# A decode kernel's tail: 22 extra TensorE products, and an output in two column halves instead of four quarters

## The chip, the cores and the metric

The kernel runs on one core of one Trainium2 chip. The metric is device time in microseconds (us). The time before is 196.53 us, the median of three runs (196.53 to 196.76).

## The reference

One decode step for four sequences. A layer norm of `x` (4 x 512) feeds two branches whose results are added to `x`: attention over the last W = 4096 cached positions with 32 query heads in 8 key/value groups, and a gated feed-forward block.

```
xn = _layernorm(x)
q  = xn @ wq                                  # 4 x 4096, 32 heads of 128
k, v = the last 4096 positions of the caches  # 8 groups, 4 query heads each
o  = softmax(q k^T / sqrt(128)) v             # 4 x 4096
out = x + o @ wo + (silu(xn @ w_gate) * (xn @ w_up)) @ w_down
```

All inputs and the output are bf16. Weights and caches together are 81 MB, which are read once.

## The kernel before, in words

SyncE's queue loads everything in one fixed order: `wq`, `w_gate`, `w_up`, then for each of the eight key/value groups 4 MB of keys and 4 MB of values into two buffers each (`kbuf`, `vbuf`), then `w_down` (into `wg_sb`), then `wo` (into the first `kbuf`, free by then). `wo` comes in five chunks of its 32 row blocks, `ROWS`: blocks 0-15, 16-21, 22-28, 29-30 and 31. Each chunk has its own semaphore, `d_wo[0]` to `d_wo[4]`. All five are issued at L249, long before the end, and land in order.

TensorE's program for a key/value group is: transpose the keys (L418), multiply them with the queries (L427), sum and weight the values (L518, L436), shift the scores (L535) and fold partial sums (L539). ScalarE and VectorE copy, take the maxima and exponentials. This loop is not touched by the change.

After the last group comes the tail (block `t_tail`), which is straight code. TensorE works in order, so each of its waits holds up everything behind it:

- The attention result of all groups, `oT`, is transposed (L559) and spread by four products (L562). VectorE turns that into `oP` with four instructions (L384, L388) and signals `s_opc`. Meanwhile TensorE multiplies `guT` with `w_down` into `part_ps` (L569, 14 products).
- TensorE waits for `s_opc` and `d_wo[0]`, then multiplies `oP` with `wo` row blocks 0 to 21 (L577, `EARLY` = 22 products of 512 columns). At block 16 it waits for `d_wo[1]`. These products go to four groups of 32 partitions in turn (`32 * k`, `k = (j + 3) % 4`). Products on different groups run beside one another.
- VectorE copies the lower 64 partitions of `part_ps` to `part` (L391), ScalarE the upper 64 (L271). Each adds one to `s_ptc`.
- TensorE waits for both, folds the four partition groups of `part` into `acc_ps` with an fp32 matrix `fold` (L582), and adds row blocks 22 to 31 directly (L589), with waits for `d_wo[2]`, `d_wo[3]`, `d_wo[4]` at blocks 22, 29 and 31. `acc_ps` is one PSUM bank, `ps_S[2]`. The four column quarters of the output stand in its four partition groups, so each row block takes four products of 128 columns.
- After `s_acc`, VectorE casts quarters 0 and 1 to bf16 into `y` (L394), ScalarE quarters 2 and 3 (L274), 4 x 128 each. SyncE waits for both and writes `y` out (L251).

Two tiles matter for the change beside these: `ones` (128 x 128 of ones, bf16) and `P` (the exponentials, bf16), both last written long before the tail. `ps_kt[1]` is a PSUM bank that the loop uses for transposed keys, and that the tail does not use. In the profile's names, `kbuf<-in_A_wo_dram` is a `wo` chunk's transfer, `ps_s` any of the four `ps_S` banks, `PEld` the load of a product's stationary matrix.

Of the kernel before, what the change touches and what calls it, by code (L numbers as in the profile page):

```python
# [10 lines left out]
def bass_parallel_sum__sliding_block_cached__swiglu_ffn__decode_kernel(  # L11
# [12 lines left out]
    B, _, D = A_x.shape  # L24
    _, HKV, Sk, Dh = A_k_cache.shape
# [10 lines left out]
    NC = D // 128  # L36
# [19 lines left out]
    WO = KB[0][:].rearrange("p t d -> p (t d)").rearrange("p (j n) -> p j n", n=D)  # L56
# [11 lines left out]
    P = sb("p", [128, NT, CQ], BF16)  # L68
# [16 lines left out]
    OP = sb("oP", [128, 32, 32], BF16)  # L85
    guT = sb("guT", [128, NF, 32], BF16)
    part = sb("part", [128, D], FP32)
    y = sb("y_sb", [B, D], BF16)
# [3 lines left out]
    ones = sb("ones", [128, 128], BF16)  # L92
    I48 = sb("i48", [48, CQ], FP32)
    Lsel = sb("lsel", [128, 128], BF16)
    fold = sb("fold", [128, 32], FP32)
# [6 lines left out]
    ps_S = [ps("ps_s%d" % s, [128, 512], FP32) for s in range(NB)]  # L102
    ps_kt = [ps("ps_kt%d" % s, [128, 512], FP32) for s in range(3)]
# [13 lines left out]
    part_ps = ps_S[0]  # L117
    rt_ps = kt_ps[0][:, 0, :]
    op_ps = ps_S[1][:].rearrange("p (b q j) -> p b q j", b=B, q=4)
    acc_ps = ps_S[2]  # L120

    def sem(name):
        return nc.alloc_semaphore(name=name)
# [47 lines left out]
    s_y = sem("s_y")  # L171
# [82 lines left out]
    def run_scalar(eng):  # L254
        eng.dma_start(X[:], x_ap).then_inc(d_x, 16)
        eng.wait_ge(s_var, 1)
        eng.activation(st_std[:], st_var[:], ACT.Sqrt).then_inc(s_std, 1)
        eng.wait_ge(s_q, 1)
        eng.copy(qs[:, 1, :], ps_S[1][:]).then_inc(s_qs, 1)
        eng.wait_ge(s_g, 1)  # L260
        eng.activation(ex, gate_ps[:], ACT.Exp, scale=-1.0).then_inc(s_ex, 1)
        with eng.Fori(0, HKV) as i:
            for n in BY_ACT:
                eng.wait_ge(s_tr[n], i + 1)
                eng.copy(KT[n % 8][:], kt_ps[n % 3]).then_inc(s_ev[n], 1)  # L265
            for q in range(NB):
                eng.wait_ge(s_sh[q], i + 1)
                eng.activation(P[:, q * TB:(q + 1) * TB, :], S_ps[q], ACT.Exp,  # L268
                               scale=SCALE).then_inc(s_xp[q], 1)
        eng.wait_ge(s_pt, 1)  # L270
        eng.copy(part[64:128, :], part_ps[64:128, :]).then_inc(s_ptc, 1)  # L271
        eng.wait_ge(s_acc, 1)
        for n in (2, 3):
            last = eng.copy(y[:, 128 * n:128 * n + 128], acc_ps[32 * n:32 * n + B, 0:128])  # L274
        last.then_inc(s_y, 1)

    def run_vector(eng):
        me = bass.OrderedEngineSet([eng.engine])
# [106 lines left out]
        for q in range(1, 4):  # L385
            eng.drain()
            dst = opf[:] if q < 3 else OP[:, :, 0:B].rearrange("p j b -> p b j")
            last = eng.scalar_tensor_tensor(dst, op_ps[:, :, q, :], quarter[:, q:q + 1], opf[:], ALU.mult, ALU.add)  # L388
# [1 line left out]
        eng.wait_ge(s_pt, 1)  # L390
        eng.tensor_copy(part[0:64, :], part_ps[0:64, :]).then_inc(s_ptc, 1)  # L391
        eng.wait_ge(s_acc, 1)
        for n in (0, 1):
            last = eng.tensor_copy(y[:, 128 * n:128 * n + 128], acc_ps[32 * n:32 * n + B, 0:128])  # L394
        last.then_inc(s_y, 1)

    def run_tensor(eng):
        mm = eng.matmul
# [5 lines left out]
        def now(reg, lo=1, hi=16 * HKV):  # L404
            return eng.snap(reg, min_val=lo, max_val=hi, donate=True)

        def step(reg, by, op=ALU.add):
            nc.regs_alu(reg, reg, by, op=op)
# [24 lines left out]
        def pv(e):  # L433
            for u in range(NT // 2):
                k = u % 4
                last = mm(o4_ps[32 * k:32 * k + 32, :], P[:, 2 * u:2 * u + 2, :].rearrange("p t c -> p (t c)"),  # L436
                          VB[e][:, 2 * u:2 * u + 2, :].rearrange("p t d -> p (t d)"),
                          start=(u < 4), stop=(u >= NT // 2 - 4), skip_group_check=True)
            last.then_inc(s_pv, 1)

        later = []

# [10 lines left out]
        with nc.body("t_head", valid_engines=me):  # L453
# [5 lines left out]
            for c in range(NC):  # L459
                last = eng.transpose(xT_ps[:, c * B:(c + 1) * B],  # L460
                                     xn[:].rearrange("b (p c) -> b c p", c=NC)[:, c, :], ident[0:B, 0:B])
# [5 lines left out]
            for c in range(NC):  # L467
                for j in range(2):
                    for k in range(4):
                        last = mm(ps_S[j][32 * k:32 * k + 32, :], XnT[:, c, :],  # L470
                                  WQ[:, c, 512 * (4 * j + k):512 * (4 * j + k) + 512],
                                  start=(c == 0), stop=(c == NC - 1), skip_group_check=True)
            last.then_inc(s_q, 1)
            eng.wait_ge(s_qs, 2)
            for j in range(2):
                for h in range(4):
                    last = eng.transpose(qT_ps[:, 4 * j + h, :], qs[:, j, 128 * h:128 * h + 128], ident[:])
            last.then_inc(s_qt, 1)
            for w, d, o, s_w in ((WG, d_wg, gate_ps, s_g), (WU, d_wu, up_ps, s_u)):
                wt = w[:].rearrange("p c (m t) -> p c t m", t=NF)  # L480
                eng.wait_ge(d, 16)
                for c in range(NC):
                    for k in range(4):
                        last = mm(o[32 * k:32 * k + 32, :].rearrange("p (t m) -> p t m", m=128), XnT[:, c, :],
                                  wt[:, c, T0[k]:T0[k] + 4, :], start=(c == 0), stop=(c == NC - 1), skip_group_check=True)
                last.then_inc(s_w, 1)
            eng.wait_ge(s_gu, 1)
            for t in range(4):
                last = eng.transpose(gT_ps[:, t, :], gu[:, 128 * t:128 * t + 128], ident[:])
# [9 lines left out]
        with nc.body("t_a_end", valid_engines=me):  # L499
            j = now(nx, 1, HKV)  # L500
# [3 lines left out]
        with nc.body("t_b_end", valid_engines=me):  # L504
            j = now(nx, 1, HKV)
# [3 lines left out]
        with nc.body("t_c_end", valid_engines=me):  # L509
            j = now(nx, 1, HKV)  # L510
# [3 lines left out]
        with nc.body("t_values", valid_engines=me):  # L514
            j = now(nx)
            for q in range(NB):
                eng.wait_ge(s_xp[q], j)
                last = mm(dn_ps[:], ones[:], P[:, q * TB:(q + 1) * TB, :].rearrange("p t c -> p (t c)"),  # L518
                          start=(q == 0), stop=(q == NB - 1))
            last.then_inc(s_dn, 1)  # L520
            eng.wait_ge(s_cm, j)
            eng.transpose(mx_ps, mxd[:], identf[:]).then_inc(s_mt, 1)  # L522
            eng.wait_ge(s_nm, j)

            def turn(g):
                eng.wait_ge(d_v[1 - g], eng.snap(nk[g], min_val=16, max_val=16 * HKV))
                step(nk[g], 16)
                pv(1 - g)

            by_parity("t_p", turn)  # L530
        with nc.body("t_p_end", valid_engines=me):
            j = now(nx)
            eng.wait_ge(s_dd, j)
            for q in range(NB):
                mm(S_ps[q], Lsel[:], bc(Dsh[:], TB), start=False, stop=True,  # L535
                   skip_group_check=True).then_inc(s_sh[q], 1)
            eng.wait_ge(s_oc, j)
            for e in range(2):
                last = mm(ot_ps, o4[:, 128 * e:128 * e + 128], fold[:, 16 * e:16 * e + 16],  # L539
                          start=(e == 0), stop=(e == 1), skip_group_check=True)  # L540
# [16 lines left out]
        with nc.body("t_tail", valid_engines=me):  # L557
            eng.wait_ge(s_nm, LAST + 2)
            eng.transpose(rt_ps, OT[:, 1:, :].rearrange("p r c -> p (r c)"), ident[:]).then_inc(s_rt, 1)  # L559
            eng.wait_ge(s_rn, 1)  # L560
            for b in range(B):
                m = mm(op_ps[:, b].rearrange("p q j -> p (q j)"), sel[:, b, :], Rn[:], start=(b == 0), stop=True,  # L562
                       skip_group_check=True)
            m.then_inc(s_op, 1)
            eng.wait_ge(s_guT, 1)
            eng.wait_ge(d_wd, 16)
            for t in range(NF):
                k = (t + 1) % 4
                mm(part_ps[32 * k:32 * k + 32, :], guT[:, t, :], WD[:, t, :], start=(t < 3), stop=False,  # L569
                   skip_group_check=True)  # L570
            eng.wait_ge(s_opc, 1)
            for j in range(EARLY):
                for q, (a, b) in enumerate(ROWS):
                    if a == j:
                        eng.wait_ge(d_wo[q], 16)
                k = (j + 3) % 4
                m = mm(part_ps[32 * k:32 * k + 32, :], OP[:, j, :], WO[:, j, :], start=False,  # L577
                       stop=(j >= EARLY - 4), skip_group_check=True)
            m.then_inc(s_pt, 1)
            eng.wait_ge(s_ptc, 2)  # L580
            for n in range(NC):
                mm(acc_ps[32 * n:32 * n + 32, 0:128], fold[:], part[:, 128 * n:128 * n + 128],  # L582
                   start=True, stop=False, skip_group_check=True)
            for j in range(EARLY, 32):
                for q, (a, b) in enumerate(ROWS):
                    if a == j:
                        eng.wait_ge(d_wo[q], 16)
                for n in range(NC):
                    m = mm(acc_ps[32 * n:32 * n + 32, 0:128], OP[:, j, :], WO[:, j, 128 * n:128 * n + 128],  # L589
                           start=False, stop=(j == 31), skip_group_check=True)  # L590
            m.then_inc(s_acc, 1)
            step(seen, 1)
            eng.br_lt(seen, 1, on_true="t_tail", on_false="t_end").branch_hint(loc)
        nc.switch_bb("t_end")

    run_gpsimd(nc.gpsimd)
    run_sync(nc.sync)
    run_scalar(nc.scalar)
    run_vector(nc.vector)
    run_tensor(nc.tensor)  # L600


# [26 lines left out]
```

## Time and profile before

| what | value |
|---|---|
| time, median of 3 runs | 196.53 us (196.53 to 196.76) |
| the profiled execution's own time | 196.74 us |
| its span, first to last instruction | 195.3 us |
| granted TensorE clock, mean over the span | 0.947 of full speed |
| TensorE busy | 154.2 us (79%) |
| VectorE / ScalarE busy | 115.5 us (59%) / 69.4 us (36%) |
| HBM read | 81.01 MB, 415 GB/s over the span |

Time zero is the first instruction of the span. The profiled execution takes 1.4 us more than its span, which lies before and after it. A line of the timeline gives the start, the duration, the engine, the source line, the operation, output and inputs with their shapes, how many instructions are merged into it, and in brackets the idle time before it and what ended that. In a line of the windows view, the figure before the comma is the length of the stretch, then come the busy time and count of each engine, the granted clock (1.00 is full speed), the share of time that the DMA engines were busy, and their GB/s. The duration of a product includes the time that it needs to pass through the array, so products that follow one another overlap in it.

### The profile page before, as it was taken

How to read it: one execution, taken by the hardware profiler on the slowest of the kernel's cores; microseconds unless marked ns; L12 is line 12 of the kernel's file. 1: busy time of each engine (PE TensorE's matmuls, PEld its weight loads, DVE VectorE, ACT ScalarE, POOL GpSimd, SP SyncE). 2: the span in 40 equal slices, each digit the busy share in tenths (PEclk: the TensorE clock that was granted, in tenths of full speed). 3: DMA queues.
4: the chain of work that ended last, by engine and by line, in shares of the span. 5: the costliest groups of instructions: out<-in, count | busy, mean ns of one | idle time of the engine just before them, and what ended most of it. 6: DMA issues, size and time to landing. Idle time of an engine off the chain costs nothing.

```text
span 195.3 us, 6515 instructions
## 1 busy us (share of the span) xinstructions
PE 154.2 (79%) x2912; PEld 119.6 (61%) x2912; DVE 115.5 (59%) x221; ACT 69.4 (36%) x88; POOL 8.9 (5%) x26
## 2 busy tenths in 40 slices
PE   0038945997998899899999986998599879987644
PEld 0013105985787788678778865885498758955312
DVE  4832283767667586776758673867266748672502
ACT  2003100560564347056434704660347046603002
POOL 7910000000000000000000000000000000000000
PEclk9999985999999999999999999999879999999955
DMA  6999999999999999999999999999999999999991
GB/s 222 430 431 435 423 450 443 426 436 426 433 426 436 425 430 430 430 436 430 430 443 436 430 436 430 430 430 430 430 436 430 430 430 430 430 430 384 429 404 59
DMA packets 3621, 81.09 MB, mean 415 GB/s; under 512 B 408, under 2 KB 544, under 8 KB 928
## 3 DMA queue, kind: packets, MB, share of 16 engines
q1 hardware_dynamic: 3608, 81.01, 97.1%
q8 instruction: 4, 0.07, 0.1%
q10 hardware_dynamic: 8, 0.00, 0.0%
q14 instruction: 1, 0.01, 0.0%
HBM read 81.01 MB, written 0.00 MB: 415 GB/s over the span
## 4 chain that ended last, share of the span: by engine, by line
DMA 44%; PE 40%; ACT 7%; DVE 4%; issue 2%; SPq 1%; DVEq 0%
DMA kbuf<-in_A_k_cache_dram 29%; PE ps_kt L418 20%; DMA kbuf<-in_A_wo_dram 15%; PE ps_s L427 9%; ACT kT L265 7%; PE ps_o L436 5%; PE ps_s L535 2%; DVE mxb L340 2%; PE ps_s L577 1%; PE ps_kt L522 1%; PE ps_o L539 1%; DVE mx L363 1%; PE ps_s L589 1%; DVE mxd L365 0%; SPq L237 0%
## 5 line engine op out<-in xcount | busy, mean ns | idle before, releaser
L418 PE MATMUL ps_kt<-ident,kbuf 128*128 128x128 bf16 x1024 | 71.4, 225 | 11.5 <-DMA kbuf<-in_A_k_cache_dram 7.8
L418 PEld LDWEIGHTS ps_kt<-ident,kbuf 128*128 128x128 bf16 x1024 | 60.7, 101 | 19.2 <-DMA kbuf<-in_A_k_cache_dram 8.3
L336 DVE COPY kT<-ps_kt 128x1024 bf16<-128x1024 bf16 x80 | 52.2, 687 | 21.5 <-PE ps_kt L418 20.7
L265 ACT COPY kT<-ps_kt 128x1024 bf16<-128x1024 bf16 x48 | 47.8, 1013 | 45.6 <-PE ps_kt L418 45.6
L268 ACT ACTIVATE p<-ps_s 128x512 bf16<-128x512 f32 x32 | 16.5, 603 | 44.4 <-PE ps_s L535 44.4
L340 DVE TENSOR_REDUCE mxb<-ps_s 128x16 f32<-128x512 f32 x32 | 22.1, 692 | 13.1 <-PE ps_s L427 11.5
L427 PE MATMUL ps_s<-qT,kT 128*128 x1024 | 29.4, 169 | 0.0
L427 PEld LDWEIGHTS ps_s<-qT,kT 128*128 128x128 bf16 x1024 | 27.8, 96 | 0.2
L436 PE MATMUL ps_o<-vbuf,p 128*32 128x256 bf16 x576 | 17.4, 273 | 1.5 <-DMA vbuf<-in_A_v_cache_dram 0.8
L436 PEld LDWEIGHTS ps_o<-vbuf,p 128*32 128x32 bf16 x576 | 15.1, 97 | 3.5 <-issue 3.2
L518 PE MATMUL ps_kt<-p,ones 128*128 128x512 bf16 x36 | 9.7, 378 | 0.2
L535 PE MATMUL ps_s<-dsh,lsel 128*128 128x512 bf16 x36 | 9.4, 382 | 0.0
L470 PE MATMUL ps_s<-vbuf,xnT 128*32 128x512 bf16 x32 | 3.6, 630 | 5.5 <-DMA vbuf<-in_A_wq_dram 5.5
L344 DVE TENSOR_REDUCE dsum<-ps_kt 128x16 f32<-128x512 f32 x9 | 6.2, 692 | 1.5 <-PE ps_kt L518 1.3
L522 PE MATMUL ps_kt<-identf,mxd 128*128 128x128 f32 x9 | 2.8, 316 | 5.0 <-DVEq L366 5.0
L350 DVE TENSOR_TENSOR oT<-ps_o,rden 128x16 f32 (+1 forms) x9 | 1.6, 175 | 8.9 <-PE ps_o L539 8.9
L522 PEld LDWEIGHTS ps_kt<-identf,mxd 128*128 128x128 f32 x9 | 1.3, 139 | 8.4 <-DVEq L366 8.4
L539 PEld LDWEIGHTS ps_o<-fold,o 128*128 128x128 f32 x36 | 5.4, 190 | 1.3
L460 PE MATMUL ps_s<-ident,xn 4*128 4x4 bf16 x4 | 0.3, 166 | 7.1 <-DVE xn L298 7.1
L577 PE MATMUL ps_s<-kbuf,oP 128*32 128x512 bf16 x22 | 2.8, 623 | 3.8 <-DMA kbuf<-in_A_wo_dram 3.8
L470 PEld LDWEIGHTS ps_s<-vbuf,xnT 128*32 128x32 bf16 x32 | 1.3, 140 | 7.0 <-issue 7.0
L271 ACT COPY part<-ps_s 64x512 f32<-64x512 f32 x1 | 0.6, 580 | 13.5 <-PE ps_s L577 13.5
(92 smaller groups left out, 76.7 us busy)
## 6 DMA issues: line engine op xcount, KB each, us to landing
kbuf<-in_A_k_cache_dram SPq DMA_DIRECT2D x8, 4096.0 KB, 26.6
vbuf<-in_A_v_cache_dram SPq DMA_DIRECT2D x8, 4096.0 KB, 28.5
vbuf<-in_A_wq_dram SPq DMA_DIRECT2D x1, 4096.0 KB, 12.3
kbuf<-in_A_wo_dram SPq DMA_DIRECT2D x1, 2048.0 KB, 30.1
wg_sb<-in_B_w_gate_dram SPq DMA_DIRECT2D x1, 1792.0 KB, 16.1
wu_sb<-in_B_w_up_dram SPq DMA_DIRECT2D x1, 1792.0 KB, 19.9
wg_sb<-in_B_w_down_dram SPq DMA_DIRECT2D x1, 1792.0 KB, 25.8
kbuf<-in_A_wo_dram SPq DMA_DIRECT2D x1, 896.0 KB, 33.2
```

The lines of the kernel that those rows point to most:

```text
L265: eng.copy(KT[n % 8][:], kt_ps[n % 3]).then_inc(s_ev[n], 1)
L268: eng.activation(P[:, q * TB:(q + 1) * TB, :], S_ps[q], ACT.Exp, scale=SCALE).then_inc(s_xp[q], 1)
L336: eng.tensor_copy(KT[n % 8][:], kt_ps[n % 3]).then_inc(s_ev[n], 1)
L340: eng.tensor_reduce(mxb[:, q, :], S_ps[q].rearrange("p t c -> p c t"), AX.X, ALU.max)
L344: eng.tensor_reduce(dsum[:], dn_ps[:].rearrange("p (t c) -> p c t", c=CQ), AX.X, ALU.add)
L418: last = eng.transpose(kt_ps[n % 3][:, k, :], KB[g][:, 8 * n + k, :], ident[:])
L427: last = mm(S_ps[q][:, 8 * (n % 4) + k, :], KT[n % 8][:, k, :], QT[:, bass.ds(j, 1), :, :].rearrange("p o b h -> p (o b h)"), start=(n % 4 ...
L436: last = mm(o4_ps[32 * k:32 * k + 32, :], P[:, 2 * u:2 * u + 2, :].rearrange("p t c -> p (t c)"), VB[e][:, 2 * u:2 * u + 2, :].rearrange(" ...
L518: last = mm(dn_ps[:], ones[:], P[:, q * TB:(q + 1) * TB, :].rearrange("p t c -> p (t c)"), start=(q == 0), stop=(q == NB - 1))
L522: eng.transpose(mx_ps, mxd[:], identf[:]).then_inc(s_mt, 1)
L535: mm(S_ps[q], Lsel[:], bc(Dsh[:], TB), start=False, stop=True, skip_group_check=True).then_inc(s_sh[q], 1)
L539: last = mm(ot_ps, o4[:, 128 * e:128 * e + 128], fold[:, 16 * e:16 * e + 16], start=(e == 0), stop=(e == 1), skip_group_check=True)
```

## The change

It does two things, both in the tail. First, 22 products are put into TensorE's program whose results nothing reads: `ones` (128 x 128) times 512 columns of `P`, into `ps_kt[1]`. There are 15 ahead of the wait for `d_wo[0]`, 3 ahead of the wait for `d_wo[1]`, 2 ahead of the wait for `s_ptc`, and 2 after the fold products, ahead of the wait for `d_wo[2]`. Second, the output is summed in two column halves of 256 instead of four quarters of 128. Half 0 stands in partitions 0-31 of bank `ps_S[2]`, half 1 in partitions 32-63 of bank `ps_S[3]`. The fold takes two products instead of four, each late row block two instead of four. VectorE casts half 0 with one instruction, ScalarE half 1 with one.

```
-    acc_ps = ps_S[2]
+    acc_ps = [ps_S[2][0:32, 0:D // 2], ps_S[3][32:64, 0:D // 2]]
+    spin_ps = ps_kt[1][:]
...
         eng.wait_ge(s_acc, 1)
-        for n in (2, 3):
-            last = eng.copy(y[:, 128 * n:128 * n + 128], acc_ps[32 * n:32 * n + B, 0:128])
-        last.then_inc(s_y, 1)
+        eng.copy(y[:, D // 2:], acc_ps[1][0:B, :]).then_inc(s_y, 1)
...
         eng.wait_ge(s_acc, 1)
-        for n in (0, 1):
-            last = eng.tensor_copy(y[:, 128 * n:128 * n + 128], acc_ps[32 * n:32 * n + B, 0:128])
-        last.then_inc(s_y, 1)
+        eng.tensor_copy(y[:, 0:D // 2], acc_ps[0][0:B, :]).then_inc(s_y, 1)
...
+        def spin(n):
+            for _ in range(n):
+                mm(spin_ps, ones[:], P[:, 0:32, :].rearrange("p t c -> p (t c)"), start=True, stop=True)
...
                     if a == j:
+                        spin((15, 3)[q])
                         eng.wait_ge(d_wo[q], 16)
...
             m.then_inc(s_pt, 1)
+            spin(2)
             eng.wait_ge(s_ptc, 2)
-            for n in range(NC):
-                mm(acc_ps[32 * n:32 * n + 32, 0:128], fold[:], part[:, 128 * n:128 * n + 128],
-                   start=True, stop=False, skip_group_check=True)
+            for h in range(2):
+                mm(acc_ps[h], fold[:], part[:, 256 * h:256 * h + 256], start=True, stop=False, skip_group_check=True)
+            spin(2)
             for j in range(EARLY, 32):
...
-                for n in range(NC):
-                    m = mm(acc_ps[32 * n:32 * n + 32, 0:128], OP[:, j, :], WO[:, j, 128 * n:128 * n + 128],
+                for h in range(2):
+                    m = mm(acc_ps[h], OP[:, j, :], WO[:, j, 256 * h:256 * h + 256],
                            start=False, stop=(j == 31), skip_group_check=True)
```

The code order on TensorE shows where the new products stand. The first place is the start of the `wo` part, from the products with `w_down` (`guT`) on. Before:

```order
L569 MATMUL ps_s<-wg_sb,guT 32x512 x13
L577 MATMUL ps_s<-kbuf,oP 32x512 [waits d_wo0,s_opc]
L577 MATMUL ps_s<-kbuf,oP 32x512 x15
L577 MATMUL ps_s<-kbuf,oP 32x512 [waits d_wo1]
L577 MATMUL ps_s<-kbuf,oP 32x512 x5
```

At the same place after the change, with L442 the new products and L581 what was L577:

```order
L572 MATMUL ps_s<-wg_sb,guT 32x512 x13
L442 MATMUL ps_kt<-p,ones 128x512 [waits s_opc]
L442 MATMUL ps_kt<-p,ones 128x512 x14
L581 MATMUL ps_s<-kbuf,oP 32x512 [waits d_wo0]
L581 MATMUL ps_s<-kbuf,oP 32x512 x15
L442 MATMUL ps_kt<-p,ones 128x512 x3
L581 MATMUL ps_s<-kbuf,oP 32x512 [waits d_wo1]
L581 MATMUL ps_s<-kbuf,oP 32x512 x5
```

The wait for `s_opc` has moved from the first `wo` product to the first of the 15 new ones: these start only when `oP` is written, and the `wo` products are queued behind them.

The second place is the end of TensorE's program, from the fold on. Before:

```order
L582 MATMUL ps_s<-part,fold 32x128 [waits s_ptc]
L582 MATMUL ps_s<-part,fold 32x128 x3
L589 MATMUL ps_s<-kbuf,oP 32x128 [waits d_wo2]
L589 MATMUL ps_s<-kbuf,oP 32x128 x27
L589 MATMUL ps_s<-kbuf,oP 32x128 [waits d_wo3]
L589 MATMUL ps_s<-kbuf,oP 32x128 x7
L589 MATMUL ps_s<-kbuf,oP 32x128 [waits d_wo4]
L589 MATMUL ps_s<-kbuf,oP 32x128 x3
```

After, with L587 for the fold and L594 for the late row blocks:

```order
L442 MATMUL ps_kt<-p,ones 128x512 x2
L587 MATMUL ps_s<-part,fold 32x256 [waits s_ptc]
L587 MATMUL ps_s<-part,fold 32x256
L442 MATMUL ps_kt<-p,ones 128x512 x2
L594 MATMUL ps_s<-kbuf,oP 32x256 [waits d_wo2]
L594 MATMUL ps_s<-kbuf,oP 32x256 x13
L594 MATMUL ps_s<-kbuf,oP 32x256 [waits d_wo3]
L594 MATMUL ps_s<-kbuf,oP 32x256 x3
L594 MATMUL ps_s<-kbuf,oP 32x256 [waits d_wo4]
L594 MATMUL ps_s<-kbuf,oP 32x256
```

Products of the fold and of the late row blocks are half as many and twice as wide. Two new ones stand ahead of the fold's wait, two between the fold and the late blocks.

## The prediction

> **What bounds the kernel now.** I read the page's slices first, then the timeline of the last 11 us, then the windows for the clock there. In the page, the 40 slices of the span show the granted clock and the DMA engines.
>
> ```profile
> span 195.3 us, 6515 instructions
> PEclk9999985999999999999999999999879999999955
> DMA  6999999999999999999999999999999999999991
> ```
>
> The transfers fill the span up to the last slice, so until then nothing that an engine does matters unless it holds a transfer back. The change touches only what follows the last key/value group, where the clock is 5, half speed. The timeline shows that stretch: what TensorE (PE, PEld), VectorE (DVE) and ScalarE (ACT) do, and in brackets what they waited for.
>
> ```profile
> 184.55 0.77 DVE L388 SCALAR_TENSOR_TENSOR oP<-ps_s,quarter,opf 128x128 bf16<-128x128 f32 x1
> 187.98 2.82 PE L577 MATMUL ps_s<-kbuf,oP 128*32 128x512 bf16 x22 [3.78 <-DMA kbuf<-in_A_wo_dram]
> 188.36 0.18 PEld L577 LDWEIGHTS ps_s<-kbuf,oP 128*32 128x32 bf16 x4 [0.25 <-issue]
> 188.79 0.18 PEld L577 LDWEIGHTS ps_s<-kbuf,oP 128*32 128x32 bf16 x4 [0.25 <-issue]
> 189.77 0.13 PEld L577 LDWEIGHTS ps_s<-kbuf,oP 128*32 128x32 bf16 x6 [0.80 <-DMA kbuf<-in_A_wo_dram]
> 190.85 0.68 DVE L391 COPY part<-ps_s 64x512 f32<-64x512 f32 x1 [5.53 <-PE ps_s L577]
> 190.85 0.58 ACT L271 COPY part<-ps_s 64x512 f32<-64x512 f32 x1 [13.47 <-PE ps_s L577]
> 191.59 0.66 PE L582 MATMUL ps_s<-part,fold 128*32 128x128 f32 x8 [0.78 <-DVE part L391]
> 191.97 1.13 PEld L589 LDWEIGHTS ps_s<-kbuf,oP 128*32 128x32 bf16 x40 [0.19 <-DMA kbuf<-in_A_wo_dram]
> 192.02 1.29 PE L589 MATMUL ps_s<-kbuf,oP 128*32 128x128 bf16 x40
> 192.99 0.11 PEld L589 LDWEIGHTS ps_s<-kbuf,oP 128*32 128x32 bf16 x4
> 193.35 0.53 ACT L274 CAST y_sb<-ps_s 4x128 bf16<-4x128 f32 x2 [1.92 <-PE ps_s L589]
> 193.35 0.58 DVE L394 CAST y_sb<-ps_s 4x128 bf16<-4x128 f32 x2 [1.82 <-PE ps_s L589]
> 193.96 0.35 SPq L251 DMA_DIRECT2D out_dram<-y_sb  x1
> ```
>
> TensorE waits for `wo` chunk 0 until 187.9, for chunk 1 until 189.7 and for chunk 2 until 191.9. The last chunk lands with the end as well. SyncE's timeline and the list of DMA issues give its time:
>
> ```profile
> 159.20 0.91 SPq L249 DMA_DIRECT2D kbuf<-in_A_wo_dram  x2
> kbuf<-in_A_wo_dram SPq DMA_DIRECT2D x1, 128.0 KB, 33.3
> ```
>
> The second of these two issues starts at about 159.20 + 0.91 / 2 = 159.65, and 33.3 us later is 192.95. The last four weight loads start at 192.99. TensorE alone would have come to them at the same time: ten rounds of four products, with 0.107 us between rounds (1.29 us less one product of 0.31, by nine), bring the tenth to 192.02 + 9 x 0.107 = 192.98. So transfer and TensorE tie here, and a faster TensorE by itself gains nothing ahead of 192.95. Only what follows can shrink: a product, the casts (0.58 us), the store.
>
> **The change, part by part.**
>
> *The casts.* VectorE's two of 128 columns take 0.28 each and become one of 256. By columns: 512 of them take 0.68 (L391), 128 take 0.28, so 1.05 ns per column, and 256 take 0.28 + 128 x 0.00105 = 0.41. A copy of that width stands in the rows of the groups by form:
>
> ```profile
> L348 DVE COPY o<-ps_o 128x256 f32<-128x256 f32 x1 | 0.4, 425 | 1.9 <-PE ps_o L436 1.9
> L436 PE MATMUL ps_o<-vbuf,p 128*32 128x256 bf16 x64 | 1.9, 273 | 0.8 <-DMA vbuf<-in_A_v_cache_dram 0.8
> L535 PE MATMUL ps_s<-dsh,lsel 128*128 128x512 bf16 x4 | 1.0, 382 | 0.0
> L589 PE MATMUL ps_s<-kbuf,oP 128*32 128x128 bf16 x40 | 1.3, 313 | 0.0
> ```
>
> I take 0.41 (0.43 is the other end). ScalarE's becomes 0.26 + 128 x (0.58 - 0.26) / 384 = 0.37 and stays under it. The gain is 0.58 - 0.41 = 0.17 us, on the path.
>
> *Width of the late products.* Ten rounds of two products of 256 columns replace ten of four of 128. At full clock the 64 products of L436, 256 columns in four groups, take 16 rounds in 1.9 us, (1.9 - 0.27) / 15 = 0.11 per round: the same as 0.107 at half clock and half the width. The last one lasts 0.27 instead of 0.31. The fold takes 192.02 - 191.59 = 0.43 until the late products start, and likewise stays 0.43 at full clock. At half clock both would double: 0.43 + 1.07 = 1.5 us more. So this half of the change leans on the clock.
>
> *The 22 products.* One of 128 x 512 at full clock follows another after (1.04 - 0.38) / 3 = 0.22 us; I use 0.216, as the 14 products of L569 have it:
>
> ```profile
> 183.39 0.81 PE L569 MATMUL ps_s<-wg_sb,guT 128*32 128x512 bf16 x10
> 182.05 0.17 DVE L350 TENSOR_TENSOR oT<-ps_o,rden 128x16 bf16<-128x16 f32 x1 [0.89 <-PE ps_o L539]
> 182.28 0.10 PEld L559 LDWEIGHTS ps_kt<-ident,oT 128*128 128x128 bf16 x1 [0.25 <-DVE oT L350]
> ```
>
> These ten end two rounds and one product after their start: (0.81 - 0.38) / 2 = 0.215. At half clock it is 188.79 - 188.36 = 0.43. TensorE follows VectorE by 182.28 - 182.22 = 0.06.
>
> At full clock throughout, the path runs so. `oP` is written at 185.32, the first new product starts at 185.38, and 15 take 3.24: 188.62. Chunk 0 has landed (187.9), so 0.7 us of them is not covered by the wait. The 16 `wo` products take 4 x 0.216 = 0.86, to 189.48; the next 3 new ones 0.65, to 190.13. Chunk 1 has landed (189.7), 0.4 us uncovered. Two rounds of `wo` products then start at 190.13 and 190.35; the last ends 0.38 later at 190.73, before it was 190.81. VectorE copies from 190.77 to 191.45, the next two new products lie under that copy and cost nothing. The fold starts at 191.51 and is through at 191.94. The last two new products take 0.43, to 192.37; chunk 2 has landed (191.9), so they are all uncovered. Ten rounds from there: the tenth starts at 192.37 + 9 x 0.107 = 193.33, after chunk 4 (192.95), and ends at 193.60. The casts start at 193.65 and end at 194.06, before 193.93.
>
> The sum is +0.30 (start of the casts) - 0.17 (casts) = +0.13 us. What the clock gains, the uncovered new products spend. The profiled execution took 196.74 us, its span 195.3; with the sum 196.87. The median is 0.21 lower, so I state 196.53 + 0.13 = **196.66**.
>
> *The clock.* All this holds if the clock stays up. The windows around the place where it fell, and around earlier changes of it:
>
> ```profile
> 184.80:185.00 0.20, 0.00 (x0) 0.00 (x0) 0.20 (x1) 0.00 (x0) 0.00 (x0) 0.74 0.97 410
> 27.50:28.00 0.50, 0.00 (x0) 0.00 (x0) 0.43 (x2) 0.00 (x0) 0.00 (x0) 0.88 0.15 66
> 34.50:35.00 0.50, 0.50 (x10) 0.50 (x8) 0.40 (x2) 0.00 (x0) 0.00 (x0) 0.79 0.15 66
> 116.63:120.04 3.41, 1.85 (x28) 1.00 1.05 452
> 137.11:140.52 3.41, 1.11 (x18) 1.00 1.05 452
> 140.52:143.93 3.41, 3.41 (x36) 0.50 1.05 452
> 181.48:184.90 3.42, 2.40 (x25) 1.00 0.98 419
> 188.31:191.72 3.41, 2.63 (x26) 0.50 0.79 312
> ```
>
> A mean of 0.74 in 184.80 to 185.00 puts the fall at 184.90; likewise 0.88 puts one at 27.88, and 0.79 a rise at 34.71. From 27.88 to 34.71 are 2 x 3.41 us, from 34.71 to 184.90 are 44 x 3.41. So the clock is decided at the ends of stretches of 3.41 us on a fixed grid. It fell after one with 1.11 us busy, kept after one with 1.85, rose after one with 3.41, did not rise after one with 2.63 (77%). It fell after 181.48 to 184.90 although 2.40 us were busy there, most of it with products 32 columns wide; so narrow ones seem to count less.
>
> At 184.90 the new products have not started. If the grid lies in the next execution as in this one, the clock falls before the first of them. If the grid lies elsewhere, it falls only when a stretch ends between about 184.75 (earlier, it takes in the wide products of L535 up to 181.66) and 185.5 (later, it takes in enough of the new ones): 0.75 of 3.41, 22%. One trace shows the grid once; nothing in it ties the grid to the program's start, so I take the second as likelier.
>
> The Trainium skill, TensorE: Matmul & The Clock Gate, "What's actually happening", says that the window is free-running and doesn't reset when a kernel starts; no run here shows it yet. The same section says that TensorE goes to half clock after at least one idle window of about 3.4 us. The trace disagrees: it fell 0.7 us after the last product, in a stretch that was 70% busy. By that rule the 1.2 us of idle time ahead of the new products could never drop the clock, and the sum would be the +0.13 with certainty.
>
> **The rivals.**
>
> *The clock falls first, and the new products run at half speed* (slower). Place: 184.90 to 188.31. From 185.38, 2.93 / 0.43 = 6.8 products are done at 188.31; that stretch is 86% busy, between 77% (no rise) and 100% (rise). If it rises there, the other 8.2 take 1.77, to 190.08 instead of 188.62. Nothing later has slack, so all of 1.46 reaches the end: 196.66 + 1.46 = 198.1. It decides as soon as the fall precedes 185.4. For it: in this trace the fall does. Against: the grid's place. The skill's same section has the rise after at least one busy window of about 3.4 us; the stretch from 140.52 agrees.
>
> *The clock falls and 86% are not enough.* Then it rises at 191.72: the 15 last until 191.79, 3.17 late, 199.8. For it: 77% did not suffice. A later rise would be worse still, since the halves then double too.
>
> *The transfers come late against TensorE* and cover the new products. If the last chunk lands 0.4 us later against `oP` than in this trace, before is later by that, while the change waits for the chunk and no more: then only what follows it counts, -0.17 for the casts and -0.04 for the last product, 196.3. For it: the three runs spread by 0.23 us. Against: the queue is full throughout, so `oP` and the chunks shift together. It is also the most that the change can gain at all.
>
> **How the numbers follow.** A measurement of this kernel tells 0.2%, 0.39 us, from no change. Full clock: 0.54; the sum there is uncertain by about 0.3 (0.43 for the casts, the spacing of 15 products, shifts of chunks), so 0.46 lie within the bound, 0.07 slower, 0.01 faster. Late transfers: 0.12, of which 0.09 same, 0.03 faster. Fall and one stretch: 0.22, fall and two: 0.12, all slower. Faster 0.04, same 0.55, slower 0.41. The range from 196.2 to 198.4 leaves out the two-stretch case, the upper edge of the one-stretch case and a little below, together about 0.2. The likeliest case by itself spans 196.4 to 197.0.
>
> **What would show it.** Right: the granted clock stays 1.00 from 182 to 193, the 15 new products end near 188.6, the copies of `part` start near 190.8, the casts near 193.65, one cast lasts 0.41. The first rival: a clock of 0.50 between 185 and 188.3, and copies near 192.2. The second: copies after 193.9. Wrong altogether: full clock and yet an end more than 0.4 us away from 194.1 for the casts, which would mean that new products delay or overlap the others differently than their spacing says, or that chunks land elsewhere.

## The result

The changed kernel takes 198.72 us (median of nine runs, 197.23 to 199.2); before takes 196.53 (nine runs, 196.47 to 196.76). The ratio is 1.0095 with a 95% interval of 1.0066 to 1.0124: it is slower by about 1%. The forecast was no change, 196.66. What came is its first rival, "The clock falls first, and the new products run at half speed", and about half a microsecond on top. The nine runs are of two kinds (see below), and the median is one of the longer kind.

The profiled execution took 199.11 us, its span is 197.5. These are its page's span and clock, then the timeline of its tail; L442 are the new products, L581 the products with `wo` that were L577, L587 the fold, L594 the late row blocks.

```profile
span 197.5 us, 6508 instructions
PEclk9999985999999999999999999999789999999789
```

```profile
184.40 0.77 DVE L388 SCALAR_TENSOR_TENSOR oP<-ps_s,quarter,opf 128x128 bf16<-128x128 f32 x1
185.23 5.10 PE L442 MATMUL ps_kt<-p,ones 128*128 128x512 bf16 x15 [1.17 <-DVE oP L388]
187.19 0.15 PEld L442 LDWEIGHTS ps_kt<-p,ones 128*128 128x128 bf16 x1 [0.28 <-issue]
187.61 0.15 PEld L442 LDWEIGHTS ps_kt<-p,ones 128*128 128x128 bf16 x1 [0.27 <-issue]
190.26 1.05 PE L581 MATMUL ps_s<-kbuf,oP 128*32 128x512 bf16 x16
191.24 0.82 PE L442 MATMUL ps_kt<-p,ones 128*128 128x512 bf16 x3
191.99 0.61 PE L581 MATMUL ps_s<-kbuf,oP 128*32 128x512 bf16 x6
192.64 0.68 DVE L391 COPY part<-ps_s 64x512 f32<-64x512 f32 x1 [7.47 <-PE ps_s L581]
193.38 0.63 PE L587 MATMUL ps_s<-part,fold 128*32 128x256 f32 x4 [0.24 <-DVE part L391]
193.94 0.60 PE L442 MATMUL ps_kt<-p,ones 128*128 128x512 bf16 x2
194.47 1.27 PE L594 MATMUL ps_s<-kbuf,oP 128*32 128x256 bf16 x20
195.78 0.41 DVE L393 CAST y_sb<-ps_s 4x256 bf16<-4x256 f32 x1 [2.46 <-PE ps_s L594]
```

TensorE no longer waits for a chunk of `wo` anywhere: no row of L581 or L594 has a DMA in brackets. The first of the 15 starts 0.06 after `oP`, but its successors come 0.42 apart, at half clock, and the `wo` products start at 190.26 instead of 187.98. All that follows is late by 1.8 to 2.5 us; the casts start at 195.78 instead of 193.35. The windows give the place of the clock's steps:

```profile
185.00:185.50 0.50, 0.27 (x2) 0.92 0.77 324
188.50:189.00 0.50, 0.50 (x3) 0.67 1.04 430
182.00:185.42 3.42, 1.93 (x21) 1.00 0.97 413
185.42:188.83 3.41, 3.41 (x9) 0.50 0.98 406
```

By 0.92 and 0.67 the clock fell at 185.42 and rose at 188.83, 3.41 later. Nine of the 15 start before the rise, the last eight of them 0.427 apart. The other six start from 188.87 on, 0.216 apart, so 6 x 0.216 = 1.30 brings them to 190.17. The `wo` products start 0.09 after that; what this 0.09 is, the run with six ahead shows.

### The profile page after: what moved, and what is told of

It is laid out like the page before. It is cut to its first block, busy times and chain, and to the rows that moved or that the text cites. A ratio compares the mean times of both kernels' runs of the same rounds, so it can differ in the third digit from the quotient of the medians.

```text
span 197.5 us, 6508 instructions
## 1 busy us (share of the span) xinstructions
PE 160.0 (81%) x2910; PEld 121.7 (62%) x2910; DVE 115.1 (58%) x220; ACT 69.2 (35%) x87; POOL 8.9 (4%) x26
## 4 chain that ended last, share of the span: by engine, by line
PE 44%; DMA 40%; ACT 7%; DVE 5%; issue 2%; SPq 1%; DVEq 0%
DMA kbuf<-in_A_k_cache_dram 28%; PE ps_kt L416 20%; DMA vbuf<-in_A_v_cache_dram 11%; PE ps_s L425 9%; ACT kT L267 7%; PE ps_o L434 6%; PE ps_kt L442 3%; PE ps_s L538 2%; DVE mxb L340 2%; PE ps_o L542 1%; PE ps_kt L525 1%; PE ps_s L581 1%; DVE mx L363 1%; PE ps_s L594 1%; DVE mxd L365 0%
## 5 line engine op out<-in xcount | busy, mean ns | idle before, releaser
L521 PE MATMUL ps_kt<-p,ones 128*128 128x512 bf16 x36 | 9.7, 378 | 0.2
L442 PE MATMUL ps_kt<-p,ones 128*128 128x512 bf16 x22 | 7.1, 474 | 1.2 <-DVE oP L388 1.2
L442 PEld LDWEIGHTS ps_kt<-p,ones 128*128 128x128 bf16 x22 | 2.3, 117 | 5.8 <-issue 3.4
```

Of the source, the lines that this page charges most:

```text
L442: mm(spin_ps, ones[:], P[:, 0:32, :].rearrange("p t c -> p (t c)"), start=True, stop=True)
```

## The experiments

TensorE's clock does not take the same course in every execution, so the spans of single runs are given beside the medians. Each ratio is to runs of the kernel before on the same chip. Where nothing else is said, an edit is to the changed kernel.

### The change again

No edit.

> The changed kernel unaltered, to see how often the clock falls ahead of the new products. Theory (the clock's grid lies by chance against the program; where a stretch ends between about 184.7 and 185.5 us the clock falls before the first new product): executions of two kinds, those with a fall near 198.1 to 199, those without near 196.7, and in a profile with a fall at half clock 7 to 8 of the 15 products take 0.43 us each. Rival (the grid is tied to the program, so the fall always comes): one kind only, all near 199.

Six runs: 198.44 us, ratio 1.0080 (1.0061 to 1.0099). There are two kinds: spans of 197.3 to 197.5 (three runs) and of 195.9 to 196.1 (three). The first nine runs divide likewise: five of 197.4 to 197.7 and four of 195.9 to 196.3. So eight of fifteen are of the longer kind. The windows of one of those:

```profile
184.80:185.00 0.20, 0.00 (x0) 0.94 0.96 410
188.00:188.50 0.50, 0.50 (x3) 0.61 0.99 410
34.50:35.00 0.50, 0.50 (x9) 0.50 (x7) 0.37 (x2) 0.00 (x0) 0.00 (x0) 0.71 0.30 131
```

The clock fell at 184.97 and rose at 188.39; the last row is an earlier rise, at 34.79, and is used below. The theory holds for the two kinds, but the shorter kind, of which no trace was kept, was not at the expected 196.7: its times are 197.2 to 198.4.

### The halves without the products

```
-                        spin((15, 3)[q])
...
-            spin(2)
...
-            spin(2)
```

> The two column halves and their single casts, without any of the 22 products. Theory: nothing holds the clock, it falls near 184.9 as before and stays at half, so the fold takes 0.85 instead of 0.43 us and ten rounds of 256 columns 2.13 instead of 1.07; casts start near 194.8, one cast lasts 0.41; time about 196.5 + 1.3 = 197.8. Rival (the width of the late products does not matter, the new products alone cost): 196.3, the cast's gain of 0.17 alone.

197.93 us, ratio 1.0051 (1.0034 to 1.0069), as the theory has it. Twelve runs: ten with spans of 196.3 to 196.7, two of 195.1 and 195.2 at 196.41 and 196.51, whose mean clock, 0.965, is the highest of the twelve. In the profile of one of the ten the clock fell later than expected, at 189.05 instead of 184.9, and stayed at half:

```profile
191.52 1.07 PE L585 MATMUL ps_s<-part,fold 128*32 128x256 f32 x4 [0.78 <-DVE part L391]
192.37 2.35 PE L591 MATMUL ps_s<-kbuf,oP 128*32 128x256 bf16 x20
194.76 0.41 DVE L393 CAST y_sb<-ps_s 4x256 bf16<-4x256 f32 x1 [3.30 <-PE ps_s L591]
```

The fold takes 0.85 until the late products start, these last 2.35 instead of 1.29, and the casts start at 194.76 (expected 194.8). The halves by themselves lose 1.3 us where the clock is at half from the fold on.

### Six products ahead, so that the clock stays up

```
+            spin(6)
             eng.wait_ge(s_opc, 1)
```

> The change with 6 more such products ahead of the wait for oP, so that TensorE is busy from 184.0 to 185.3 and all 22 stand where they stood. Theory (the loss is the clock's fall ahead of the first of the 15): the clock stays at 1.00, the 15 take 3.24 us, they end near 188.6, casts start near 193.65, time 196.66 (the sum of the prediction for full clock), and the spread of the times shrinks. Rival (the loss is the number of products in TensorE's queue, whatever the clock): as slow as the change or slower by 6 x 0.22 = 1.3 us, 199 to 200.

198.03 us, ratio 1.0062 (1.0049 to 1.0075), spans 195.9 to 196.7. Neither expectation holds for the time. The clock stayed at 1.00 and the `wo` products started where the prediction's sum had them, at 188.64, but the casts did not:

```profile
184.00 4.71 PE L442 MATMUL ps_kt<-p,ones 128*128 128x512 bf16 x21
188.64 1.05 PE L582 MATMUL ps_s<-kbuf,oP 128*32 128x512 bf16 x16
189.62 0.82 PE L442 MATMUL ps_kt<-p,ones 128*128 128x512 bf16 x3
190.37 0.61 PE L582 MATMUL ps_s<-kbuf,oP 128*32 128x512 bf16 x6
191.03 0.68 DVE L391 COPY part<-ps_s 64x512 f32<-64x512 f32 x1 [5.83 <-PE ps_s L582]
191.76 0.62 PE L588 MATMUL ps_s<-part,fold 128*32 128x256 f32 x4 [0.24 <-DVE part L391]
192.32 0.61 PE L442 MATMUL ps_kt<-p,ones 128*128 128x512 bf16 x2
192.86 1.27 PE L595 MATMUL ps_s<-kbuf,oP 128*32 128x256 bf16 x20
194.17 0.41 DVE L393 CAST y_sb<-ps_s 4x256 bf16<-4x256 f32 x1 [2.46 <-PE ps_s L595]
```

From 188.64 on, four rounds last 0.98 instead of 0.86, three new products 0.75 instead of 0.65, the fold 0.56 instead of 0.43, two new products 0.54 instead of 0.43. Each time full-width products (128 columns of the stationary matrix) follow narrow ones (32) or the reverse, about 0.11 us is added, together 0.46. That is a new theory, tested below.

The runs of this kernel also took 1.5 to 2.4 us outside the span, against 1.3 in most runs of before. In its trace the list of DMA queues behind the span shows one fetch of instructions:

```profile
q8 instruction: 1, 0.02, 1.5%
```

### The 15 products moved ahead of the wait for oP

```
+            spin(15)
             eng.wait_ge(s_opc, 1)
...
-                        spin((15, 3)[q])
+                        spin((0, 3)[q])
```

> The change with its 15 products moved from behind the wait for oP to ahead of it; 22 in all, as in the change. Theory: they run at full clock from 184.0 to 187.2, under the wait for the first wo chunk (187.8), cost nothing, and the clock stays up; the 16 products with wo start near 187.9, copies of part near 190.4, the end then hangs on the last chunk (192.9), casts near 193.35 with one of 0.41: 196.3 to 196.4. Rival (number of products): 198.7 as the change.

196.59 us, ratio 1.0000 (0.9992 to 1.0009), eleven runs.

```profile
184.65 3.41 PE L442 MATMUL ps_kt<-p,ones 128*128 128x512 bf16 x15
187.99 1.05 PE L582 MATMUL ps_s<-kbuf,oP 128*32 128x512 bf16 x16
193.51 0.41 DVE L393 CAST y_sb<-ps_s 4x256 bf16<-4x256 f32 x1 [2.46 <-PE ps_s L595]
```

The same 22 products cost nothing where 15 of them lie under VectorE's work and the wait for the first chunk, so their number was not the loss. The clock stayed up in the profile. The casts start at 193.51 instead of the expected 193.35: the two products behind the fold and the changes of width are in the path.

### Before, with six products

```
+            spin(6)
             eng.wait_ge(s_opc, 1)
```

The edit is to the kernel before; quarters and casts stay, and `spin` is defined as in the change.

> The kernel before with 6 such products ahead of the wait for oP, quarters kept; nothing else. They lie under the waits for oP and for the first wo chunk, so the span stays at 195.2 to 195.3 us or gets 0.2 shorter with the clock up. Theory (six more products push TensorE's code over what had been fetched, and it fetches 16 KB more behind its last instruction, as in the trace of the run with 28 products): the time outside the span grows from 1.3 to 1.6 or more, up to 2.4, median 196.9 to 197.6. Rival (the time outside the span has nothing to do with the code's length): 1.3 outside, 196.4 to 196.6.

196.52 us, ratio 0.9996 (0.9987 to 1.0005), 1.3 us outside the span in nine runs of eleven. The theory on the code's length falls for this kernel. The clock stayed up from 142.9 to 194.1, and yet the gain is nothing that can be measured:

```profile
187.96 1.05 PE L584 MATMUL ps_s<-kbuf,oP 128*32 128x512 bf16 x16 [2.39 <-DMA kbuf<-in_A_wo_dram]
189.75 0.61 PE L584 MATMUL ps_s<-kbuf,oP 128*32 128x512 bf16 x6 [0.75 <-DMA kbuf<-in_A_wo_dram]
191.93 1.26 PE L596 MATMUL ps_s<-kbuf,oP 128*32 128x128 bf16 x40 [0.37 <-DMA kbuf<-in_A_wo_dram]
193.25 0.57 DVE L395 CAST y_sb<-ps_s 4x128 bf16<-4x128 f32 x2 [2.17 <-PE ps_s L596]
```

The late products last 1.26 although the clock is full, where the kernel with quarters and 22 products (below), which waits for no chunk, needs 0.74. So TensorE is faster, but waits for the last chunks; the casts start 0.10 earlier.

### Fifteen products ahead and no others

```
+            spin(15)
             eng.wait_ge(s_opc, 1)
...
-                        spin((15, 3)[q])
...
-            spin(2)
...
-            spin(2)
```

> The two halves and 15 products, all ahead of the wait for oP; the other 7 are gone. Theory (a product of full width among products 32 columns wide costs about 0.11 us more than its own 0.216 on each side, and those behind the fold were uncovered): the clock stays up, wo products start near 187.9 and 189.75, copies near 190.4, the late products wait for chunks 2 and 4, casts start near 193.3 and end near 193.72: span 195.0 to 195.1, time 196.35 to 196.45. Rival (the halves or the casts cost something themselves): no better than with all 22 moved or kept, 196.6.

196.41 us, ratio 0.9987 (0.9979 to 0.9996), spans 194.8 to 195.5: a small gain, as expected. The profiled run is the longest of the eleven: its clock fell at 192.20, and the late products, 1.27 in the runs above, took 1.97.

```profile
192.00:192.50 0.50, 0.50 (x12) 0.70 0.10 33
191.79 1.97 PE L592 MATMUL ps_s<-kbuf,oP 128*32 128x256 bf16 x20 [0.18 <-DMA kbuf<-in_A_wo_dram]
```

### Narrow products instead of full width

```
-                mm(spin_ps, ones[:], P...
+                mm(spin_ps[0:32, :], ones[:, 0:32], P...
```

The edit is to the kernel with the 15 moved ahead.

> The run with the 15 products moved ahead, but each of the 22 is 32 columns wide (ones cut to 32 columns, the results in 32 partitions), same 512 columns of P, so each should still take 0.216 us. Theory on the change between widths (its cost comes from waiting until the narrow products have left the array before a full-width weight load): the extra 0.11 us per change is gone or much smaller, so where the clock is full the copies start near 190.2 and the late products wait for chunk 2 alone. Theory on the clock (narrow products count by their width): it falls at the end of a stretch between 185 and 188.5 and stays at half, casts then near 194.8, time 197.8 to 198.0. Rivals: same gaps as with full width; and a clock that stays up, 196.4 to 196.6.

196.34 us, ratio 0.9987 (0.9977 to 0.9997), spans 194.9 to 195.3. The extra time at a change is gone:

```profile
188.09 1.05 PE L582 MATMUL ps_s<-kbuf,oP 128*32 128x512 bf16 x16 [0.24 <-DMA kbuf<-in_A_wo_dram]
188.97 0.81 PE L442 MATMUL ps_kt<-p,ones 128*32 128x512 bf16 x3
189.88 0.61 PE L582 MATMUL ps_s<-kbuf,oP 128*32 128x512 bf16 x6
190.32 0.59 PE L442 MATMUL ps_kt<-p,ones 128*32 128x512 bf16 x2
```

Four rounds now last 0.88 (0.98 with full width) and two 0.44 (0.54: 190.37 to 190.91 in the run with six ahead). The theory on the clock fell: it stayed up with narrow products.

### The products with four quarters

```
+                        spin((15, 3)[q])
...
+            spin(2)
...
+            spin(2)
```

The edit is to the kernel before, with `spin` defined as in the change.

> The kernel before with the change's 22 products in the change's places (15, 3, 2, 2), but the output in four quarters and two casts on each engine. Theory: the clock falls ahead of the first of the 15 in about half the executions, as in the change; at full clock afterwards, fold and late products of 128 columns take half as long (0.22 and 0.54 instead of 0.43 and 1.07), the casts 0.58 instead of 0.41: span about 0.6 shorter than the change's, 196.9 with the fall, 195.3 without. The code is 22 products longer than before, so 0.3 to 1.1 us more outside the span: 198.2 to 199.0 and 196.8 to 197.6. Rival (the halves are what slows the change): 196.5.

197.47 us, ratio 1.0051 (1.0031 to 1.0071). Again two kinds: five runs with spans of 196.9 to 197.1, seven of 195.4 to 196.0, both within 0.7 of what was expected, and 0.4 to 0.5 less than the change's. The time outside the span was 1.3 to 1.7; the 0.3 to 1.1 more that was expected there came in part of the runs at most. In the profile the clock fell at 185.03. At full clock four narrow groups are faster than two, once nothing is waited for:

```profile
185.00:185.50 0.50, 0.23 (x1) 0.53 0.97 410
194.17 0.74 PE L598 MATMUL ps_s<-kbuf,oP 128*32 128x128 bf16 x40
194.96 0.57 DVE L395 CAST y_sb<-ps_s 4x128 bf16<-4x128 f32 x2 [1.74 <-PE ps_s L598]
```

### Narrow, without the two behind the fold

```
-            spin(2)
             for j in range(EARLY, 32):
```

The edit is to the kernel with narrow products.

> The run with 32-column products without the two behind the fold: 15 ahead of the wait for oP, 3 ahead of the second wo chunk, 2 under the copies, 20 in all, halves kept. Theory (at full clock and without changes of width TensorE is ahead of the last chunk, which lands at 192.8 to 193.0; only what follows it is left): late products wait for chunk 4, casts start at its landing plus 0.35, one cast of 0.41, span 194.9 to 195.0, time 196.25 to 196.35, 0.15% under before and no more. Rival (there is more to gain from a TensorE that is earlier still): 196.1 or less.

196.30 us, ratio 0.9986 (0.9977 to 0.9995), spans 194.9 to 195.2, as the theory has it. It is the fastest of all by its median, though not to be told from the two kernels at 0.9987.

```profile
187.90 1.05 PE L582 MATMUL ps_s<-kbuf,oP 128*32 128x512 bf16 x16 [0.16 <-DMA kbuf<-in_A_wo_dram]
191.89 1.30 PE L594 MATMUL ps_s<-kbuf,oP 128*32 128x256 bf16 x20 [0.19 <-DMA kbuf<-in_A_wo_dram]
193.23 0.41 DVE L393 CAST y_sb<-ps_s 4x256 bf16<-4x256 f32 x1 [2.22 <-PE ps_s L594]
```

### Six ahead and all 22, narrow

The edit for narrow products, made to the kernel with six ahead.

> The run with 6 products ahead and the change's 22 in their places, all 32 columns wide. Theory (the prediction's sum for full clock was right but for the changes between widths): with them gone the 16 wo products start near 188.6, copies of part near 190.75, late products near 192.3, casts near 193.6, against 194.17 with full width; span 195.3 to 195.4, if the clock stays up. Rival (the 0.5 us came from elsewhere): casts near 194.2, span 195.9.

197.20 us, ratio 1.0030 (1.0018 to 1.0042), spans 195.3 to 196.0. The clock stayed up; copies start at 190.62, late products at 191.82, and the casts here:

```profile
193.54 0.41 DVE L393 CAST y_sb<-ps_s 4x256 bf16<-4x256 f32 x1 [2.24 <-PE ps_s L595]
```

That is 193.54 against 193.65 in the prediction's sum and 194.17 with full width: the missing half microsecond was the changes of width. `oP` was ready at 185.17 here, 0.15 before the 185.32 of the sum, and with that the sum has the copies at 190.62 and the casts at 193.50. Two marks of the expectation were missed: the first `wo` product starts at 187.73 (188.6 expected) and the late ones at 191.82 (192.3), since narrow new products and `wo` products of other column groups run beside one another in this trace: the last of the 15 starts only at 188.26. By the copies and the casts that gained nothing. The time outside the span was 1.3 to 2.9, and its trace too has a fetch of instructions behind the end. The two kernels with 28 new products have that fetch. The one with quarters and 22 new products, which has the longest tail of all (107 products), hasn't, nor has before with six. What decides it stays open.

## Why the prediction was right in part and wrong in part

The number was no change, and the kernel became 1% slower, where the prediction counted 0.2% as a difference. Two steps failed: the choice of the case in which the clock stays up, and the size of the term for the 22 products.

**The bound** was right. The last chunk and TensorE tie, and no kernel came more than 0.14% under before, whatever the clock (the ratios 0.9987, 0.9987 and 0.9986).

**The casts** were right: one of 256 columns takes 0.41 on VectorE and 0.36 on ScalarE, for 0.41 and 0.37.

**The width of the late products** was right in both directions. At full clock they last 1.27 to the end of the last; at half clock the halves lose 1.3 us, which is the 1.5 of the prediction less the 0.17 of the casts.

**The 22 products at full clock** were mis-sized. Their own spacing of 0.216 held: in the run with six ahead, 21 of them take 4.64, from 184.00 to 188.64, which is 21 x 0.216 and 0.10 more. That the `wo` products start at 188.64 there, for 188.62 in the sum, is in part luck: the 15 begin at 184.00 + 6 x 0.216 = 185.30 instead of 185.38, and a change of width makes up for it. For the sum took a product to start where the one before left off, and each change between full width and 32 columns costs 0.11 more. Four such changes lie in the path behind 188.6, and the term +0.13 becomes +0.6: casts at 194.17 for 193.65. They end at 194.58, more than 0.4 from 194.1 at full clock, which the prediction had named as a sign that it is wrong about how the new products delay the others. The shorter runs of the change fit that, with spans of 195.9 to 196.3 against 195.3 in before.

**The clock** is the step that turned the sign. Its mechanism and place were right: the three falls seen after the prediction, at 185.42, 184.97 and 185.03, all lie in the band from 184.75 to 185.5, and each time the clock rose one stretch later. What failed is how often: "0.75 of 3.41, 22%" took the grid to lie anywhere with equal chance, the two cases with a fall got 0.34 together, and the number was that of the case without. By the spans, the clock fell in eight of fifteen runs of the change and in five of twelve with quarters, together 13 of 27; by 22% it would be six. The rise near 35 us, worked out as in the prediction, gives the grid in each of twelve traces. Three of these rows, of the change, of the six ahead and of the 15 moved ahead:

```profile
35.00:35.50 0.50, 0.50 (x10) 0.50 (x8) 0.50 (x1) 0.00 (x0) 0.00 (x0) 0.77 2.12 885
37.00:38.00 1.00, 1.00 (x22) 0.82 0.91 393
36.00:37.00 1.00, 1.00 (x16) 0.72 1.17 492
```

They put it at 35.23, 37.36 and 36.56; all twelve lie between 34.71 and 37.36, so the grid is not tied to the program. The band for a fall, 44 stretches earlier, is 34.56 to 35.31, and five of the twelve are in it (34.71, 34.79, 34.84, 35.19, 35.23). By 22% two or three would be; twelve traces are too few to call that more than chance. So either the grid does not lie evenly, or the band is wider than was reckoned. No trace of the shorter kind was kept, so which of the two holds stays open. As it is, a median over runs falls into the longer kind as often as not. The Trainium skill, TensorE: Matmul & The Clock Gate, "What's actually happening", says that the window is free-running and doesn't reset when a kernel starts; these traces agree that it moves, by up to 2.65 us.

**The price of the first rival** was 198.1. Against the run with six ahead, where the clock stayed up, the casts of the profiled execution start 195.78 - 194.17 = 1.6 later, for the 1.46 that was reckoned. The grid lies half a microsecond later than in before, so that the whole stretch of 3.41 at half clock falls on products instead of 2.93 of it, and half of 3.41 is 1.7. With 0.5 for the changes of width and 0.17 more outside the span (1.61 for 1.44) that is 196.66 + 1.6 + 0.5 + 0.17 = 198.9, and the profiled execution, less the 0.21 by which the one of before exceeded its median, is 199.11 - 0.21 = 198.9. The stated range reached to 198.4. By the ratio the change stands at 198.40, by its median, 198.72, above that. That it lies at the edge is luck: the edge came from the chances of the cases, and the half microsecond that was missing is in none of them.

**The second and third rival** did not occur: a stretch that is 86% busy (2.94 of 3.42 us from 184.97 to 188.39 in the second trace of the change) sufficed for the rise, and no trace shows a last chunk that came late against `oP`: it lands 7.6 after `oP` in before and 6.3 to 7.6 after it in the twelve traces. That the two shift together held for eight of them. In the other four, in which the clock was at half for one or two stretches from 158 or 159 us on, `oP` lies 0.5 to 1.3 nearer to the chunk.

## What to carry to other kernels

Work that only keeps TensorE's clock up must start in the gap itself, ahead of the wait that opens it, not behind: the same 15 products cost about 2 us behind the wait for `oP` (198.72 us) and nothing ahead of it (196.59). Count them at the slow clock first, since they run there if they come too late, and against the transfer that they wait for. Where a transfer bounds the end, a faster clock and a shorter cast gain only what follows the last chunk, here 0.3 us at most.

## What the runs showed of the hardware

- A product 128 columns wide next to products 32 columns wide costs 0.10 to 0.13 us beyond its own spacing at full clock, on each side; with fillers 32 columns wide this is gone (0.88 for 0.98, 0.44 for 0.54). That the weight load has to wait for the narrow products is argued, not shown.
- A stretch need not be idle for the clock to fall at its end: 1.93 of 3.42 us busy dropped it in the change. Nor does busy time alone decide: 1.72 kept it in the kernel before with six products, and 1.72 dropped it at 192.20 in the kernel with fifteen ahead and no others:

```profile
183.84:187.26 3.42, 1.72 (x12) 1.00 0.94 394
188.78:192.20 3.42, 1.72 (x22) 1.00 0.66 257
```

  The first of these two stretches holds six full-width products, the second narrow ones alone, which would fit the prediction's guess that narrow ones count less. But they do count: a stretch of narrow ones alone that was 3.31 of 3.41 busy, 183.80 to 187.21 in the last run, kept the clock. The rule stays open.
- The time outside the span, 1.3 us in most runs, was up to 2.9 in single runs of kernels with 22 to 28 new products, and 2.4 in one run of before. No experiment here told what decides it.
